# Token sums, first weight splits and the range check's count: three moves in an instruction order

## The chip, the core and the metric

The kernel runs on one core of a Trainium2 chip. Five engines work side by side, each through its own queue in order: PE (TensorE, matrix products), DVE (VectorE), ACT (ScalarE), POOL (GpSimd) and SP (SyncE), which here only starts DMAs. An engine that waits for a semaphore holds up all that stands behind it in its queue. The metric is device time in microseconds (us), the median of several executions; smaller is better. TensorE's clock is granted at one of two levels, 2.4 GHz (1.00 in the views) or 1.2 GHz (0.50).

## What is computed

The reference runs a recurrent attention over 2 x 8 heads of 768 steps, then a feed-forward with an ELU, then four experts that all tokens pass, weighted by shares:

```python
def _moe_ref(x, w_in, w_out):
    h = x @ w_in
    g = np.where(h > 0.0, h, alpha * (np.exp(np.minimum(h, 0.0)) - 1.0))
    return (g @ w_out).astype(np.float32)

def _moe2_ref(x, domain_probs, w1, w2):
    p = domain_probs / (domain_probs.sum(-1, keepdims=True) + 1e-09)
    for e in range(E):
        h = np.maximum(x @ w1[e], 0.0)
        out += p[:, e:e + 1] * (h @ w2[e])
```

There are 1536 tokens of 384 values. The feed-forward is 384 to 2048 to 384; each expert is 384 to 1024 to 384, in float32.

## The kernel before

**Precision.** Every matrix operand is split into a high and a low part: ACT copies the value with rounding (high), DVE or POOL subtracts that from the value (low, line 153). Each product is three passes: high x high, high x low, low x high (`PASSES`). So a matmul that reads a fresh activation waits in its first pass for ACT's copy and in its second for the subtraction.

**The feed-forward** is written as 48 steps, in the hand-written list `ORDER` (lines 67 to 91). Step n takes a quarter of the hidden width (n // 12), a block of 512 tokens (n // 4 % 3) and a slice of 128 hidden values (n % 4). Its tokens: `h` is the first product (9 matmuls, L364, into one bank of PSUM) and ACT's relu and exp on it (L367, L368, into a tile `e` of which there are 2); `e` is DVE's ELU (L372) and ACT's high copy into a tile `hl` (3 of them); `el` is the low part (L153, D on DVE, P on POOL); `z` is the second product (9 matmuls, L384, into three banks); `dr` adds a quarter's sums to the tokens x2 (L393). The last quarter has its dr39, dr43 and dr47 for blocks 0, 1 and 2; these also write the high (ACT) and low (POOL) parts of the new tokens. The first product of a later step needs a bank that an earlier `e` or `dr` has read. Tokens `wl`, `wa`, `wb`, `wc` load and split the feed-forward's weights.

**The experts** follow in `experts`. It gives every piece of work a key, its place in a row of products, and issues all in order of the keys; the feed-forward's last steps (the `lead`, behind the `|` in `ORDER`) are put in with negative keys, 3 for each `h` and `z`. The row begins with `plain`: the first products of two units (u = 0, 1) as 108 matmuls (L577) over blocks 0, 1, 2. From row 36 on the units 2 to 15 take 15 products (L547) each instead of 18, on sums of token blocks and sums of weight blocks; second products (L599) stand between. The sums of tokens are the list `TOKENS` (L527, DVE, 16 of them; "q", "s0", "s2", "v" and six more live in a pool `first` that closes at row `SPREAD`), their high parts L530 (ACT), their low parts L535 or L153. The sums of weight blocks are L465 (POOL, 6 for a unit), their high parts ACT, their low parts POOL (`sums`, L153). The blocks come by DMA into 2 tiles `blocks` (L456).

**The range check.** The program takes each decay chunk's smallest and largest value (L625), compares them with bounds (`judged`, two L629), counts with one small matmul (L631), and a flag decides at the very end whether a slow exact path runs. With these inputs it doesn't.

Of the kernel before, what the change touches and what calls it, by code (L numbers as in the profile page):

```python
# [32 lines left out]
TERMS = 18  # L33
EDGE = 120
AHEAD = 6
SPREAD = 8

# [18 lines left out]
AS_IS = {6: (1, 2), 3: (2, 2), 14: (2, 1)}  # L58
PLACE = {0: 9, 8: 10, 9: 11, 12: 12, 1: 13, 11: 14, 4: 0, 7: 3, 10: 6, 13: 1, 5: 4, 2: 2}


TOKENS = [("q", (1, 1), (2, 1)), (0, "q", (0, 1)), ("s0", (0, 0), (0, 1)), (8, (1, 0), (1, 1)), ("s2", (2, 0), (2, 1)),
          ("v", 8, "s2"), (9, "v", "s0"), (12, 8, (2, 1)), (1, 12, "s0"), (11, 12, (0, 1)),
          (4, 0, (1, 2)), (7, 4, (0, 2)), (10, 9, (2, 2)), (13, "q", (1, 2)), (5, "v", (2, 2)), (2, 10, (0, 2))]


ORDER = """
# [18 lines left out]
z28 z25 h34 wa13D el29P e34 z29 z26 h33 h35 z27 e33 el34P wa28D dr27A h30 z32 wa29D wb13D e35 el33P wb28P z33 wa14D e30  # L86
h31 el35D wb14P wl15 wb29P wc13P wc28D e31 wl31 el30D h36 el31P wc29P z34 wa30D wa15D e36 h40 el36P z30 z35 h41 wb30P
e40 dr35D wc14P wb15D h37 z31 wa31D el40P e37 e41 wb31P wc15P el37P dr31D z40 h42 h38 e38 wc30D el41P e42 h43 z36 e43
z37 h39 wc31P el42P el43P el38D z41 e39 h44 z42 z38 e44 el39D z39 el44D dr39D z43 dr43D h45 e45 h46 el45D z44 e46 h47
el46D z45 e47 z46 el47D z47 dr47A  # L90
""".split()


# [1 line left out]
def kernel_body(ctx, tc, wkr, vv, uu, w_in, w_out, w1, w2, dp, out):  # L95
# [336 lines left out]
    def experts(guard=False, lead=(), switch=None):  # L432
# [5 lines left out]
        def at(key, run, *args):  # L438
            events.append((key, len(events), run, args))
# [187 lines left out]
        def judged():  # L627
            for m, op in enumerate((ALU.is_lt, ALU.is_gt)):
                nc.vector.tensor_single_scalar(ends[:, m], ends[:, m], SAFE[m], op)  # L629
            n = pools["psum"].tile([P, 512], F32, tag="bank", name="chain_n")[0:1, 0:2 * NCH]  # L630
            nc.tensor.matmul(n, lhsT=ones, rhs=ends.rearrange("q a b -> q (a b)"), start=True, stop=True)  # L631
            nc.vector.tensor_reduce(flag, n, mybir.AxisListType.X, ALU.max)


        n, keys = 0, []
# [8 lines left out]
        row = [("plain", f, b, j) for b in range(3) for f in range(4) for j in range(3)]  # L644
# [8 lines left out]
        place = {g: n for n, g in enumerate(row)}  # L653
# [17 lines left out]
        for e in range(4):  # L671
            for b in range(3):
                at(max(SPREAD + 1, place["second", 2 * e, b, 0, 0] - 60), load_share, e, b)
        for u in range(16):
            n = place["product", u, 0] if u > 1 else -20 + 10 * u
            at(n - 75, load_blocks, u)
            if u < 2:
                for i in (0, 3):
                    at(n - 20 + i, split_hi, u, 0, 6, 6, i, 3)
                    at(n - 19 + i, split_lo, u, 0, 6, 6, i, 3)  # L680
                continue
            for i, s in enumerate(SUMS):
                at(n - (50 if u > 2 else 60) + 2 * i, sum_blocks, u, *s)
            for part, at_first, size, k in ((0, 9, 8, n - (34 if u > 2 else 45)), (1, 0, 7, n - 10)):
                for i in (0, 4):
                    at(k + i, split_hi, u, part, at_first, size, i, min(4, size - i))
                    at(k + i + 1.4, split_lo, u, part, at_first, size, i, min(4, size - i))
        for h in range(8):
            n = place["second", h, 0, 0, 0]
# [4 lines left out]
                    at(max(0, n - 37 + 6 * m + 3 * q), second_lo, h, m, q)  # L694
        made = {}
        for i, t in enumerate(TOKENS):
            made[t[0]] = -15.5 + 1.2 * i if i < 10 else 0.5 + 1.1 * (i - 10)
            at(made[t[0]], sum_tokens, i < 10, *t)
        for r, n in PLACE.items():
            k = max(made[r] + 0.7, {0: 11.5, 1: 23.5, 2: 35.5}[n % 3] + 0.9 * (n // 3) if n < 9 else -99)  # L700
            at(k, tokens_hi, r)
# [5 lines left out]

        at(SPREAD, spread_out)
        if guard:
            for c in range(NCH):  # L710
                at(70 + 33 * c - 30, load_guard, c)
                for m in range(2):
                    at(70 + 33 * c + 12 * m, guarded, c, m)
            at(len(row) - 20, judged)
        with tc.manual_schedule():
            for _, _, run, args in sorted(events, key=lambda v: v[:2]):
                run(*args)
# [5 lines left out]
    def switch():  # L723
        m1.close()
        late_pools(late)

    experts(guard=True, lead=ORDER[cut + 1:], switch=switch)
    late.close()
    early.close()
# [32 lines left out]
    with tc.If(some > 0, preferred_fallthrough_block=False):  # L762
        with ExitStack() as es:
            gp = es.enter_context(tc.tile_pool(name="gp", bufs=2))
            sp = es.enter_context(tc.tile_pool(name="sp", bufs=1))
            pools["psum"] = es.enter_context(tc.tile_pool(name="psum", bufs=8, space=PSUM))
            pick = sp.tile([P, 256], F32, name="pick")
            nc.gpsimd.memset(pick, 0.0)
            nc.gpsimd.memset(pick[0:64, 127:128], 1.0)
            nc.gpsimd.memset(pick[64:128, 191:192], 1.0)  # L770
            sts = [sp.tile([P, D, NPAIR], F32, name=f"st{b}") for b in range(2)]
            for st in sts:
                nc.gpsimd.memset(st, 0.0)
            for i in range(NCH):
                recur(i, gp)
        work.clear()
        bank_pool(m0)
        with ExitStack() as es:
            feed_forward_pools(es)
            for q in range(4):  # L780
                do(f"{t}{16 * m + 4 * q + n}" + "D" * (t in ("wa", "wb")) + "P" * (t == "wc") for m in range(2) for n in range(4) for t in ("wl", "wa", "wb", "wc"))
                for n in range(4 * len(BLOCKS) * q, 4 * len(BLOCKS) * (q + 1)):
                    do((f"h{n}", f"e{n}", f"el{n}D", f"z{n}") + (f"dr{n}A",) * (n % 4 == 3))
        with ExitStack() as es:
            early_pools(es)
            late_pools(es)
            experts()
        m0.close()
# [57 lines left out]
```

## Time and profile before

| | us |
|---|---|
| median of 3 runs (684.63 to 685.57) | 685.25 |
| the profiled execution's own time | 684.58 |
| its span | 682.6 |
| PE busy in the span | 641.2 (94%) |
| DVE busy | 498.1 (73%) |
| POOL busy | 397.4 (58%) |
| ACT busy | 304.0 (45%) |

PE is busy in nearly all of the span, so what counts is where it is not, and where it runs at the lower clock. The feed-forward ends, and `plain` begins, at 302.66 us; the sums and the range check are found by their lines.

### The profile page before, as it was taken

How to read it: one execution, taken by the hardware profiler on the slowest of the kernel's cores; microseconds unless marked ns; L12 is line 12 of the kernel's file. 1: busy time of each engine (PE TensorE's matmuls, PEld its weight loads, DVE VectorE, ACT ScalarE, POOL GpSimd, SP SyncE). 2: the span in 40 equal slices, each digit the busy share in tenths (PEclk: the TensorE clock that was granted, in tenths of full speed). 3: DMA queues.
4: the chain of work that ended last, by engine and by line, in shares of the span. 5: the costliest groups of instructions: out<-in, count | busy, mean ns of one | idle time of the engine just before them, and what ended most of it. 6: DMA issues, size and time to landing. Idle time of an engine off the chain costs nothing.

```text
span 682.6 us, 9079 instructions
## 1 busy us (share of the span) xinstructions
PE 641.2 (94%) x3314; PEld 521.6 (76%) x3314; DVE 498.1 (73%) x687; ACT 304.0 (45%) x581; POOL 397.4 (58%) x341
## 2 busy tenths in 40 slices
PE   6768999999999998869999999999999999999994
PEld 4657788888888877648887878878878788788873
DVE  7999997548465653876477687786977877867773
ACT  1334746657564564544552353334423533344220
POOL 5799685325341463873543487675776886744352
PEclk9989999999999999959999999999999999999998
DMA  7665651213211311001202112013121121300012
GB/s 261 193 185 165 213 201 52 61 48 99 64 47 46 99 43 48 23 1 46 86 23 86 31 54 86 15 40 97 44 72 45 34 75 32 115 1 2 0 47 98
DMA packets 20970, 50.83 MB, mean 74 GB/s; under 512 B 2680, under 2 KB 3880, under 8 KB 20916
## 3 DMA queue, kind: packets, MB, share of 16 engines
q1 hardware_dynamic: 20772, 50.15, 23.4%
q8 instruction: 28, 0.46, 0.3%
q14 instruction: 26, 0.21, 0.1%
q10 hardware_dynamic: 144, 0.00, 0.0%
HBM read 46.58 MB, written 2.38 MB: 72 GB/s over the span
## 4 chain that ended last, share of the span: by engine, by line
PE 77%; DVE 10%; POOL 5%; issue 3%; DMA 2%; ACT 1%; SPq 0%; DVEq 0%; POOLq 0%; ACTq 0%
PE second L599 25%; PE bank L364 12%; PE bank L384 12%; PE chain_a L547 8%; PE chain_b L547 4%; PE chain_p L577 4%; PE chain_c L547 3%; PE chain_d L547 3%; DVE scaled L608 2%; DVE first L527 2%; PE bank L292 1%; PE chain_e L547 1%; PE bank L285 1%; POOL kr L150 1%; PE bank L336 1%
## 5 line engine op out<-in xcount | busy, mean ns | idle before, releaser
L599 PE MATMUL second<-hl,w2s 128*128 128x512 f32 x864 | 230.5, 389 | 0.0
L599 PEld LDWEIGHTS second<-hl,w2s 128*128 128x128 f32 x864 | 162.0, 188 | 34.1 <-DVE hl L592 0.2
L613 POOL TENSOR_TENSOR x<-scaled,x 128x512 f32<-128x512 f32 x60 | 84.8, 1439 | 89.4 <-DVE scaled L608 89.4
L384 PE MATMUL bank<-hl,w 128*128 128x512 f32 x432 | 107.8, 400 | 10.2 <-DVE hl L153 7.8
L153 POOL TENSOR_TENSOR sums<-blocks,sums 128x512 fp32r<-128x512 f32 (+1 forms) x60 | 81.3, 1366 | 55.5 <-ACT sums L157 55.5
L384 PEld LDWEIGHTS bank<-hl,w 128*128 128x128 f32 x432 | 81.9, 192 | 29.9 <-DVE hl L153 9.0
L364 PE MATMUL bank<-x,w 128*128 128x512 f32 x432 | 104.0, 391 | 0.5 <-DVE e L372 0.5
L592 DVE SCALAR_TENSOR_TENSOR hl<-terms,hl 128x512 fp32r<-128x512 f32 x96 | 90.6, 947 | 13.3 <-ACT hl L589 13.3
L364 PEld LDWEIGHTS bank<-x,w 128*128 128x128 f32 x432 | 80.4, 188 | 18.6 <-DVE e L372 1.5
L465 POOL TENSOR_TENSOR blocks<-blocks 128x256 f32<-128x256 f32 x84 | 70.9, 861 | 1.7 <-DMA blocks<-in_w 0.6
L153 POOL TENSOR_TENSOR hl<-e,hl 128x512 fp32r<-128x512 f32 x25 | 34.1, 1368 | 56.3 <-ACT hl L157 56.2
L372 DVE SCALAR_TENSOR_TENSOR e<-e,bank 128x512 f32<-128x512 f32 x48 | 32.4, 681 | 43.5 <-ACT e L368 43.5
L589 ACT ACTIVATE hl<-terms 128x512 fp32r<-128x512 f32 x96 | 57.0, 624 | 15.0 <-PE second L599 10.3
L559 DVE TENSOR_TENSOR terms<-terms,chain_a 128x512 f32<-128x512 f32 x42 | 28.7, 684 | 37.9 <-PE chain_a L547 37.9
L562 ACT ACTIVATE terms<-chain_b 128x512 f32<-128x512 f32 x28 | 16.8, 598 | 83.2 <-PE chain_b L547 83.0
L562 ACT ACTIVATE terms<-chain_a 128x512 f32<-128x512 f32 x28 | 16.7, 596 | 78.4 <-PE chain_a L547 78.4
L547 PE MATMUL chain_a<-x,sums 128*128 128x512 f32 x168 | 47.2, 389 | 0.0
L608 DVE TENSOR_TENSOR scaled<-second,pr 128x512 f32<-128x512 f32 x63 | 41.2, 679 | 7.5 <-PE second L599 7.5
L157 ACT ACTIVATE hl<-e 128x512 fp32r<-128x512 f32 x48 | 30.1, 629 | 35.5 <-PE bank L384 22.4
L157 ACT ACTIVATE sums<-blocks 128x512 fp32r<-128x512 f32 (+1 forms) x60 | 35.2, 592 | 13.6 <-POOL sums L153 6.2
L367 ACT ACTIVATE e<-bank 128x512 f32<-128x512 f32 x48 | 28.4, 593 | 26.7 <-PE bank L364 14.2
L547 PEld LDWEIGHTS chain_a<-x,sums 128*128 128x128 f32 x168 | 31.5, 188 | 6.5
(117 smaller groups left out, 1013.2 us busy)
## 6 DMA issues: line engine op xcount, KB each, us to landing
kr<-in_wkr SPq DMA_DIRECT2D x12, 512.0 KB, 4.0
raw<-in_w_in SPq DMA_DIRECT2D x16, 384.0 KB, 3.5
raw<-in_w_out SPq DMA_DIRECT2D x16, 384.0 KB, 3.3
blocks<-in_w SPq DMA_DIRECT2D x16, 384.0 KB, 3.4
raw<-in_w SPq DMA_DIRECT2D x16, 384.0 KB, 4.5
v<-in_vv SPq DMA_DIRECT2D x12, 456.0 KB, 4.4
w<-in_wkr SPq DMA_DIRECT2D x12, 258.5 KB, 3.8
gw<-in_wkr SPq DMA_DIRECT2D x12, 258.0 KB, 2.8
```

Source lines behind the costliest of these rows:

```text
L153: engines[e].tensor_tensor(o, a, b.bitcast(F32), ALU.subtract)
L157: nc.scalar.activation(out=o, in_=a, func=AF.Copy)
L364: nc.tensor.matmul(ph, lhsT=wi[:, sa, f, kk, :], rhs=x[:, kk, c0:c0 + nch, sm], start=(kk == 0 and i == 0), stop=(kk == 2 and i == 2))
L384: nc.tensor.matmul(pxs[q, bl][d], lhsT=wo[:, sa, f, d * P:(d + 1) * P], rhs=b["t"][:, sm], start=(f == 0 and i == 0), stop=(f == 3 and i = ...
L465: nc.gpsimd.tensor_tensor(*(places(blocks[u], p) for p in (r, a, c)), ALU.subtract if op == "-" else ALU.add)
L547: nc.tensor.matmul(banks[c], lhsT=weights(u, r, sa), rhs=tokens(r)[:, sm], start=r in HEADS and i == 0, stop=i == 2, skip_group_check=True)
L562: nc.scalar.activation(out=new({0: 0, 6: 5, 3: 2, 5: 3, 8: 4}[r]), in_=ps, func=AF.Copy, scale=-1.0 if r in (6, 8) else 1.0)
L589: nc.scalar.activation(out=hls[f, b][:, 0], in_=results[f, b], func=AF.Relu)
L592: nc.vector.scalar_tensor_tensor(hls[f, b][:, 1], results[f, b], 0.0, hls[f, b][:, 0].bitcast(F32), ALU.max, ALU.subtract)
L599: nc.tensor.matmul(sums[d], lhsT=w[:, sa, f, d * P:(d + 1) * P], rhs=hls[4 * h + f, b][:, sm], start=f == i == 0, stop=f == 3 and i == 2)
L608: nc.vector.tensor_tensor(o, sums[d], prs[h // 2, b], ALU.mult)
L613: (nc.vector if last else nc.gpsimd).tensor_tensor(x2[:, d, s], scaled[d], x2[:, d, s], ALU.add)
```

## The change

Four numbers or lists move; no operation is added or taken away but a split of one function in two.

- The end of `ORDER`: before, the last first products are h39, h44, h45, h46, h47; now h44, h39, h46, h45, h47, each with a second product between, and block 1's sums (dr43) are taken ahead of block 0's (dr39).
- `TOKENS` begin at key -0.9 instead of -15.5, one each 1.05, and stand in another order; which of them live in the pool `first` is now a set. `SPREAD` goes from 8 to 18.
- Units 0 and 1 split their weights 40 keys earlier (-60 instead of -20), and their DMAs come 40 earlier; unit 2's weight sums go from 60 ahead to 97, its first half's split from 45 to 82, its DMA from 75 to 112.
- The comparisons of the range check go from 20 rows ahead of the end to 26; the count stays at 20.

```diff
-SPREAD = 8
+SPREAD = 18
-TOKENS = [("q", (1, 1), (2, 1)), (0, "q", (0, 1)), ("s0", (0, 0), (0, 1)), (8, (1, 0), (1, 1)), ("s2", (2, 0), (2, 1)),
...
+TOKENS = [("q", (1, 1), (2, 1)), (0, "q", (0, 1)), (4, 0, (1, 2)), (7, 4, (0, 2)), ("s0", (0, 0), (0, 1)),
...
+FIRST = {"q", "s0", "s2", "v", 0, 8, 9, 12, 1, 11}
...
-z37 h39 wc31P el42P el43P el38D z41 e39 h44 z42 z38 e44 el39D z39 el44D dr39D z43 dr43D h45 e45 h46 el45D z44 e46 h47
-el46D z45 e47 z46 el47D z47 dr47A
+z37 h44 wc31P el42P el43P el38D z41 h39 e44 e39 z42 h46 z38 z43 el44D dr43D el39D h45 z44 e45 z39 el45P dr39A e46 h47
+z45 el46D z46 e47 el47D z47 dr47A
...
         def judged():
             for m, op in enumerate((ALU.is_lt, ALU.is_gt)):
                 nc.vector.tensor_single_scalar(ends[:, m], ends[:, m], SAFE[m], op)
+
+        def counted():
             n = pools["psum"].tile([P, 512], F32, tag="bank", name="chain_n")[0:1, 0:2 * NCH]
...
-            n = place["product", u, 0] if u > 1 else -20 + 10 * u
-            at(n - 75, load_blocks, u)
+            n = place["product", u, 0] if u > 1 else -60 + 10 * u
+            at(n - (75 if u != 2 else 112), load_blocks, u)
...
-                at(n - (50 if u > 2 else 60) + 2 * i, sum_blocks, u, *s)
-            for part, at_first, size, k in ((0, 9, 8, n - (34 if u > 2 else 45)), (1, 0, 7, n - 10)):
+                at(n - (50 if u > 2 else 97) + 2 * i, sum_blocks, u, *s)
+            for part, at_first, size, k in ((0, 9, 8, n - (34 if u > 2 else 82)), (1, 0, 7, n - 10)):
...
-            made[t[0]] = -15.5 + 1.2 * i if i < 10 else 0.5 + 1.1 * (i - 10)
-            at(made[t[0]], sum_tokens, i < 10, *t)
+            made[t[0]] = -0.9 + 1.05 * i
+            at(made[t[0]], sum_tokens, t[0] in FIRST, *t)
...
-            at(len(row) - 20, judged)
+            at(len(row) - 26, judged)
+            at(len(row) - 20, counted)
```

DVE at the feed-forward's end, before, right behind step 46's ELU: step 46's low part is hl_2669, step 47's ELU is e_2682 and its low part hl_2713.

```order
L527 TENSOR_TENSOR first_2686<-x2_62 128x512
L527 TENSOR_TENSOR first_2689<-x2_62 128x512
L527 TENSOR_TENSOR first_2693<-first_2686,first_2689 128x512
L153 TENSOR_TENSOR hl_2669<-e_2642,hl_2669 128x512
L527 TENSOR_TENSOR first_2705<-first_2693,first_2666 128x512
L527 TENSOR_TENSOR first_2709<-first_2686,x2_62 128x512
L372 SCALAR_TENSOR_TENSOR e_2682<-e_2682,bank_2672 128x512
L527 TENSOR_TENSOR first_2725<-first_2709,first_2666 128x512
L527 TENSOR_TENSOR first_2729<-first_2709,x2_62 128x512
L535 SCALAR_TENSOR_TENSOR xb_1405<-first_2725,xb_1405 128x512
L535 SCALAR_TENSOR_TENSOR xb_1405<-first_2729,xb_1405 128x512
L153 TENSOR_TENSOR hl_2713<-e_2682,hl_2713 128x512
```

The same stretch of DVE now, from step 39's low part (hl_2566) to the first token sum (step 46 is hl_2669 again, step 47 hl_2704).

```order
L153 TENSOR_TENSOR hl_2566<-e_2556,hl_2566 128x512
L372 SCALAR_TENSOR_TENSOR e_2632<-e_2632,bank_2622 128x512
L393 TENSOR_TENSOR x2_62<-bank_2491,x2_62 128x512
L393 TENSOR_TENSOR x2_62<-bank_2492,x2_62 128x512
L393 TENSOR_TENSOR x2_62<-bank_2493,x2_62 128x512
L372 SCALAR_TENSOR_TENSOR e_2590<-e_2590,bank_2580 128x512
L153 TENSOR_TENSOR hl_2669<-e_2590,hl_2669 128x512
L372 SCALAR_TENSOR_TENSOR e_2682<-e_2682,bank_2672 128x512
L153 TENSOR_TENSOR hl_2704<-e_2682,hl_2704 128x512
L527 TENSOR_TENSOR first_2719<-x2_62 128x512
```

No token sum stands ahead of a low part any more but "q", which now follows the last of them.

POOL some 50 us earlier, before: the low parts of steps 36 (hl_2317), 40 (hl_2367), 37 (hl_2403) and 41 (hl_2406) among weight pieces (raw, w3, w7).

```order
L153 TENSOR_TENSOR hl_2317<-e_2295,hl_2317 128x512
L195 TENSOR_TENSOR raw_2084<-raw_2084,t_2309 128x384
L153 TENSOR_TENSOR w3_1906<-raw_2015,w3_1906 128x384
L153 TENSOR_TENSOR hl_2367<-e_2330,hl_2367 128x512
L195 TENSOR_TENSOR raw_2282<-raw_2282,t_2398 128x384
L153 TENSOR_TENSOR w3_1906<-raw_2273,w3_1906 128x384
L153 TENSOR_TENSOR hl_2403<-e_2386,hl_2403 128x512
L153 TENSOR_TENSOR hl_2406<-e_2362,hl_2406 128x512
```

POOL there now; the steps 36, 40, 37 and 41 are hl_2320, hl_2378, hl_2415 and hl_2418.

```order
L153 TENSOR_TENSOR sums_2309<-blocks_1992,sums_2309 128x384 x2
L153 TENSOR_TENSOR hl_2320<-e_2295,hl_2320 128x512
L153 TENSOR_TENSOR sums_2357<-blocks_2057,sums_2357 128x384
L195 TENSOR_TENSOR raw_2088<-raw_2088,t_2312 128x384
L153 TENSOR_TENSOR w3_1906<-raw_2017,w3_1906 128x384
L153 TENSOR_TENSOR sums_2357<-blocks_2057,sums_2357 128x384
L153 TENSOR_TENSOR hl_2378<-e_2333,hl_2378 128x512
L195 TENSOR_TENSOR raw_2282<-raw_2282,t_2410 128x384
L153 TENSOR_TENSOR w3_1906<-raw_2273,w3_1906 128x384
L153 TENSOR_TENSOR hl_2415<-e_2397,hl_2415 128x512
L465 TENSOR_TENSOR blocks_2359<-blocks_2359 128x256
L465 TENSOR_TENSOR blocks_2359<-blocks_2359 128x2x128
```

Four low parts of the units' weights (sums) came in ahead of step 40's low part, and two weight sums (L465) ahead of step 41's, which is the next row.

DVE at the range check, some 40 second products ahead of the end (- before, + now).

```order
 L608 TENSOR_TENSOR scaled<-second,pr 128x512
 L592 SCALAR_TENSOR_TENSOR hl<-terms,hl 128x512
+L629 TENSOR_SCALAR ends<-ends 128x12 x2
 L608 TENSOR_TENSOR scaled<-second,pr 128x512 x2
 L592 SCALAR_TENSOR_TENSOR hl<-terms,hl 128x512 x2
-L629 TENSOR_SCALAR ends<-ends 128x12 x2
-L632 TENSOR_REDUCE flag<-chain_n 1x1
+L634 TENSOR_REDUCE flag<-chain_n 1x1
```

The two comparisons moved up past two weighted sums (L608) and two low parts (L592); the count on PE stays at its place.

## Rows read from the trace of the kernel before

**Rows 1.** PE in order of time: start, us, instruction; in brackets idle time before it.

```profile
236.25 4.25 PE L384 MATMUL bank<-hl,w 128*128 128x512 f32 x18
240.34 2.21 PE L364 MATMUL bank<-x,w 128*128 128x512 f32 x9
242.85 2.33 PE L364 MATMUL bank<-x,w 128*128 128x512 f32 x9 [0.30 <-DVE e L372]
...
249.10 6.28 PE L364 MATMUL bank<-x,w 128*128 128x512 f32 x27
...
263.71 2.34 PE L364 MATMUL bank<-x,w 128*128 128x512 f32 x9 [0.17 <-DVE e L372]
...
271.99 4.15 PE L384 MATMUL bank<-hl,w 128*128 128x512 f32 x17 [1.64 <-DVE hl L153]
...
287.52 0.49 PE L384 MATMUL bank<-hl,w 128*128 128x512 f32 x1 [1.19 <-ACT hl L157]
289.39 2.94 PE L384 MATMUL bank<-hl,w 128*128 128x512 f32 x8 [1.37 <-DVE hl L153]
293.50 0.79 PE L384 MATMUL bank<-hl,w 128*128 128x512 f32 x1 [1.17 <-ACT hl L157]
299.08 3.78 PE L384 MATMUL bank<-hl,w 128*128 128x512 f32 x8 [4.79 <-DVE hl L153]
302.66 17.64 PE L577 MATMUL chain_p<-x,sums 128*128 128x512 f32 x74
```

**Rows 2.** Windows: length, busy PE, PEld, DVE, ACT, POOL (count), granted clock, DMA share, GB/s.

```profile
270.00:280.00 10.00, 8.36 (x37) 6.66 (x36) 7.13 (x10) 6.39 (x11) 8.30 (x7) 1.00 0.31 103
285.00:290.00 5.00, 2.44 (x10) 1.46 (x10) 4.96 (x8) 2.27 (x4) 2.58 (x3) 1.00 0.00 0
...
295.00:300.00 5.00, 0.92 (x2) 0.82 (x3) 3.93 (x4) 1.15 (x2) 1.67 (x2) 0.50 0.00 0
```

**Rows 3.** DVE in order of time, at the feed-forward's end and in `plain`.

```profile
280.11 0.95 DVE L527 TENSOR_TENSOR first<-x 128x512 f32<-128x512 f32 x1
...
286.73 1.28 DVE L527 TENSOR_TENSOR first<-x 128x512 f32<-128x512 f32 x2
...
297.26 1.77 DVE L153 TENSOR_TENSOR hl<-e,hl 128x512 fp32r<-128x512 f32 x1
...
305.97 1.78 DVE L527 TENSOR_TENSOR terms<-first,x 128x512 f32<-128x512 f32 x1
...
315.07 1.88 DVE L153 TENSOR_TENSOR x<-terms,x 128x512 fp32r<-128x512 f32 x3
```

**Rows 4.** POOL in order of time: a step's low part, a weight piece, unit 0's first splits.

```profile
240.93 1.29 POOL L153 TENSOR_TENSOR hl<-e,hl 128x512 fp32r<-128x512 f32 x1 [3.46 <-ACT hl L157]
242.18 1.02 POOL L195 TENSOR_TENSOR raw<-raw,t 128x384 int32<-128x384 int32 x1
...
266.04 1.99 POOL L153 TENSOR_TENSOR sums<-blocks,sums 128x384 fp32r<-128x384 f32 x2 [0.29 <-ACT sums L157]
```

**Rows 5.** The page's group of weight sums: count, busy us, mean ns, idle before.

```profile
L465 POOL TENSOR_TENSOR blocks<-blocks 128x256 f32<-128x256 f32 x84 | 70.9, 861 | 1.7 <-DMA blocks<-in_w 0.6
```

**Rows 6.** ACT in order of time: a step's exp, and unit 0's first high parts.

```profile
241.37 0.64 ACT L368 ACTIVATE e<-e 128x512 f32<-128x512 f32 x1
...
265.45 0.92 ACT L157 ACTIVATE sums<-blocks 128x384 fp32r<-128x384 f32 x2
```

**Rows 7.** PE at the first second products.

```profile
327.84 4.24 PE L599 MATMUL second<-hl,w2s 128*128 128x512 f32 x18
```

**Rows 8.** The range check: its comparisons on DVE, its count on PE.

```profile
658.26 1.30 DVE L629 TENSOR_SCALAR ends<-ends 128x12 f32<-128x12 f32 x2
...
659.61 0.21 PE L631 MATMUL chain_n<-ends,ones 128*1 128x24 f32 x2 [1.41 <-DVE ends L629]
```

**Rows 9.** A feed-forward weight chunk: its DMA's start on SP, its first use on DVE.

```profile
204.37 0.33 SPq L184 DMA_DIRECT2D raw<-in_w_in  x1
...
215.70 0.35 DVE L189 TENSOR_SCALAR t<-raw 128x384 int32<-128x384 int32 x1
```

More of the change, by code (lines that the diff above doesn't have):

```diff
@@ L59 @@
 PLACE = {0: 9, 8: 10, 9: 11, 12: 12, 1: 13, 11: 14, 4: 0, 7: 3, 10: 6, 13: 1, 5: 4, 2: 2}
-TOKENS = [("q", (1, 1), (2, 1)), (0, "q", (0, 1)), ("s0", (0, 0), (0, 1)), (8, (1, 0), (1, 1)), ("s2", (2, 0), (2, 1)),
-          ("v", 8, "s2"), (9, "v", "s0"), (12, 8, (2, 1)), (1, 12, "s0"), (11, 12, (0, 1)),
-          (4, 0, (1, 2)), (7, 4, (0, 2)), (10, 9, (2, 2)), (13, "q", (1, 2)), (5, "v", (2, 2)), (2, 10, (0, 2))]
+TOKENS = [("q", (1, 1), (2, 1)), (0, "q", (0, 1)), (4, 0, (1, 2)), (7, 4, (0, 2)), ("s0", (0, 0), (0, 1)),
+          (8, (1, 0), (1, 1)), ("s2", (2, 0), (2, 1)), ("v", 8, "s2"), (9, "v", "s0"), (10, 9, (2, 2)),
+          (13, "q", (1, 2)), (5, "v", (2, 2)), (12, 8, (2, 1)), (1, 12, "s0"), (11, 12, (0, 1)), (2, 10, (0, 2))]
+FIRST = {"q", "s0", "s2", "v", 0, 8, 9, 12, 1, 11}
 ORDER = """
```

## The prediction

> **What bounds the kernel now.** PE is busy in 94% of the span, so I looked first at the granted clock and at PE's busy share in slices of time, found one place in mid-kernel where both fall, then read PE in order of time there, and behind each of its waits the engine that ended it. Before 263 us PE's waits are tenths of a microsecond. From there to the first row of `plain` they are 1.64, 1.19, 1.37, 1.17 and 4.79 us, ended by DVE's low parts (L153) and by ACT's copies of ELUs that DVE gave late [rows 1]. In windows PE is busy for 2.44 of 5 us at 285, and 0.92 of 5 at 295 at half clock, while DVE is busy nearly all the time [rows 2]. So here DVE sets the pace, and what it does is sums of tokens (L527), of which the step that PE waits for has no need.
>
> How much is lost? 18 matmuls take 236.25 to 240.34, 0.227 us each, 2.045 for a group of 9 (one `h` or `z`). From 240.34 to `plain` there are 23 groups (h41, h37, z31, z40, then 19 from h42 at 249.10 on), so without any wait `plain` would start at 240.34 + 23 x 2.045 = 287.4. It starts at 302.66 [rows 1]: **15.3 us lost**. The seven waits make 10.6 of that; the matmuls at half clock (8 in 2.94 us, 8 in 3.78, one in 0.79) some 3.2; the rest is restarts.
>
> **Term 1, the old waits: -15.3.** Now no token sum stands between the ELUs and low parts of the last steps; all but one come after them. I walk the tail in the new order. When z39's last bank is done, DVE adds it (0.64), then come step 46's ELU (0.64), ACT's copy (0.7 with its hand-over), step 46's low part, step 47's ELU, ACT's copy and step 47's low part. An unhindered DVE row takes 0.64 (two in 1.28), a low part beside POOL 1.77 [rows 3]; POOL is then at block 0's three low parts, so step 46 gets 1.77, and step 47, behind them, 0.64. Sum 5.7 us. PE wants the last in z47's second matmul, three groups and 0.2 later, 6.3 us: it fits by 0.6. With 1.77 for step 47 too it would be 0.5 late; I take nothing and keep 0.5 as the bound. Each last first product (h39, h46, h45, h47) now also has second products behind it that are ready.
>
> **Term 2, new waits at 246 to 266 us: +3.2.** The price of the earlier weight splits lies on POOL. POOL now has part of the units' splitting ahead of the low parts of steps 40 and 41. ACT's copy of step 36 needs a tile `hl` that z30 frees at 236.25 + 2.05 + 0.1 = 238.4 [rows 1]. Then ACT does that copy, step 40's relu and exp, and a block's high part, 0.46 to 0.64 each, 0.57 apart on the mean [rows 6]: POOL can start the second unit-0 split at 240.7. From there POOL has no pause: split 1.0, step 36's low part 1.3, split 1.0, weight pieces 1.0 and 1.0, split 1.0, step 40's low part 1.3 [rows 4], and ends at 248.3. PE would want it in z40's second matmul, at 240.34 + 3 x 2.045 + 0.23 = 246.7 [rows 1]: **a wait of 1.65**. The old 0.30 at 242.85 is inside this: if it stays, this one is that much shorter. Then h42 wants the bank that step 37's ELU reads; its relu waited for the tile `e` that step 40's low part frees: 248.4 + 2 x 0.6 + 0.7 = 250.4, against 250.2 for z40's end: **0.25**. Then on POOL: a weight piece behind ACT's conversion (250.1 to 251.1), another to 252.1, step 37's low part to 253.4, two weight sums of 0.86 [rows 5] to 255.1, step 41's low part to 256.4. Step 38's relu waits for that, and its ELU comes at 258.5; z36's third bank needs it at 250.4 + 3 x 2.045 + 6 x 0.227 = 257.9: **0.6**. The wait for a bank at h44 (0.17 before, now at h39) stays: **0.2**. Together 2.7; a group behind a wait is 0.12 longer (2.33 against 2.21 [rows 1]), four times 0.5. Bounds: nothing, if ACT and POOL come 1.7 earlier than walked; and 1.1 more, if DVE holds up one of POOL's rows for as long as POOL held up the low part at 297.26 (1.77 - 0.64 [rows 3]).
>
> **Term 3, the clock: -0.6.** `plain` starts at half clock. Its 108 matmuls take 302.66 to 327.84, 25.2 us, against 24.5 at 0.227 [rows 1, 7]. With no long wait ahead of it this goes.
>
> **Term 4, the range check: -1.5.** PE waits 1.41 for the comparisons [rows 8], plus 0.12 for the restart. They now come six rows of three matmuls earlier, 6 x 0.68 = 4.1 us. In exchange the two of them, 1.30 us, stand ahead of two weighted sums and two low parts; those low parts are issued 5.3 rows (3.6 us) before their use. I take nothing for that, with 1.3 as the bound: the place has no row before.
>
> **Term 5, the token sums in their new place: 0, up to +6.2.** They now lie beside `plain`. From the last addition L393 (about 0.9 into `plain`) to the first low part that a second product needs, DVE has 27 rows: 15 sums, 4 low parts of second weights, 8 of tokens. PE gives them 24.5 + 0.2 - 0.9 = 23.8 us, or 0.88 for a row. What does a row take? Unhindered 0.64 [rows 3]. From 305.97 to 316.95 there were 12 in 10.98, 0.915 each; from 280.11 to 299.03 there were 17 in 18.9, 1.11 each; the first and the last of both stand in [rows 3]. The first stretch had POOL busy for about 8 of 11 us. In the new place POOL has six low parts of 1.3 and six weight sums of 0.86, 12.8 of 24 us, so I scale the excess: 0.64 + 0.275 x (0.53 / 0.74) = 0.84. 27 x 0.84 = 22.7: in time by 1.1. At 0.915 it is 0.9 late, at 1.11 it is 6.2 late. I take 0, the price of the nearest row with its cover scaled, and keep 6.2 for the range.
>
> Here the Trainium skill has a rule that speaks against the change. The row first: at 297.26 a subtraction took 1.77 instead of 0.64, 1.13 more, in a stretch in which POOL worked too [rows 3]. The page "SBUF — State Buffer", section "Who interferes with whom", says that a DVE instruction with two SBUF inputs contends with a GpSimd instruction that reads SBUF, and that whoever starts first keeps the shared ports for its whole instruction. By that rule at its worst, each of POOL's 12 instructions beside `plain` would hold up one DVE row by its whole length: 27 x 0.64 + 12.8 = 30.1, 6.3 late, and the sum below would end at 677.4 instead of 671.1. That one row agrees in size; the 12 rows from 305.97, at 0.915, do not show it for each.
>
> **Free edits.** The blocks' DMAs (384 KB) stand earlier on SP, among feed-forward weight chunks. A chunk started at 204.37 is first used at 215.70 [rows 9], 11 us later, which covers a transfer ahead of it; without that cover it would cost the transfer. `SPREAD` only delays the shares' DMA to the row where the pool `first` closes, and its readers come behind the first four second products.
>
> **The sum.** -15.3 + 3.2 - 0.6 - 1.5 + 0 = -14.2. The profiled execution would go from 684.58 to 670.4 (span 682.6 to 668.4); it lies 0.67 under the median of the runs, so the median goes from 685.25 to **671.1**.
>
> **Rivals.**
>
> 1. *The clock falls at the new wait.* PE would stand for 1.65 and 0.25 us within 4 us. For it: at 285 the engine was busy for 2.44 of 5 us, and half clock followed [rows 2]. Against: at 270.4 it waited 1.64 in one piece and the clock stayed at 1.00 [rows 1, 2]. One to three groups at half clock: 2 to 6 us, 673 to 677.
> 2. *DVE stays the bound, beside `plain`.* The sums are only moved to where the second products wait for DVE; the point is a mean row of 0.88 us. Then up to 6.2 comes back: 672 to 677.4. For it the stretch at 1.11, against it the one at 0.915 with more POOL work beside it.
> 3. *Slower than before.* The clock falls at z40 and the small waits that follow (h42, z36, h39) keep it at half up to `plain`: 19 groups x 2.045 = 38.9 more, some 710. It decides from the seventh group on (14.2 / 2.045). Against: behind z40 there would be waits of 0.6 and 0.2 in 16 us, and the window with a wait of 1.64 in it stayed at 1.00; the clock fell behind windows with PE busy for half of the time [rows 2].
> 4. *No new wait at all.* ACT and POOL come early enough at z40: 3.2 less, 668.
>
> **How the numbers follow.** Forecast 0.68, rival 1 0.10, rival 2 0.13, rival 3 0.02, rival 4 0.06, something unseen at either side 0.01. The forecast's own spread is about 1.5 us (term 2's 1.1, term 4's 1.3, term 1's 0.5, not all at once). The range of 668.0 to 676.0 takes in the forecast, rival 4 and most of rivals 1 and 2. A measurement of this kernel tells 0.2%, about 1.4 us, from no change; all but rival 3 are far beyond: faster 0.97, same 0.01, slower 0.02.
>
> **What would show it.** Right: `plain` starts near 290.5, no PE wait over 1 us from 266 to there, granted clock 1.00 throughout; a PE wait of 1 to 2 us near 247 ended by POOL's low part; no wait at the count; first second products 24.5 us after `plain`. Wrong: a wait of PE for DVE's L592 at the first second products (rival 2), a clock under 1.00 behind 247 (rival 1), no wait there (rival 4), or waits in the last six groups (term 1).

## The result and the profile after

The changed kernel takes **676.93 us** (median of 4 runs, 674.91 to 677.39), the kernel before 685.18 in the same comparison: a ratio of 0.9874, 95% interval 0.9853 to 0.9896. It is faster by 8.3 us, where 14.2 were forecast, and lies 0.9 above the range. The profiled execution took 674.91 (span 673.0).

PE in order of time: start, us, instruction, in brackets the idle time ahead of it and what ended it.

```profile
236.48 4.24 PE L384 MATMUL bank<-hl,w 128*128 128x512 f32 x18
...
244.64 2.77 PE L384 MATMUL bank<-hl,w 128*128 128x512 f32 x10
249.41 3.27 PE L384 MATMUL bank<-hl,w 128*128 128x512 f32 x8 [2.00 <-POOL hl L153]
252.48 6.76 PE L364 MATMUL bank<-x,w 128*128 128x512 f32 x27
...
286.01 6.28 PE L384 MATMUL bank<-hl,w 128*128 128x512 f32 x27
292.13 24.64 PE L577 MATMUL chain_p<-x,sums 128*128 128x512 f32 x108
316.97 0.50 PE L599 MATMUL second<-hl,w2s 128*128 128x512 f32 x1 [0.20 <-ACT hl L589]
320.05 4.15 PE L599 MATMUL second<-hl,w2s 128*128 128x512 f32 x17 [2.58 <-DVE hl L592]
324.04 0.84 PE L547 MATMUL chain_d<-x,sums 128*128 128x512 f32 x3
```

The waits of [rows 1] between 270 us and `plain` are gone: `plain` starts at 292.13 instead of 302.66, and the last three groups (27 matmuls) run in one piece. Two waits are left. One was forecast: 2.00 at z40 for POOL's low part of step 40. The other is at the very first second products, 2.58 for DVE.

Windows (length, busy PE, PEld, DVE, ACT, POOL with counts, granted clock, DMA share, GB/s):

```profile
245.00:250.00 5.00, 2.94 (x13) 1.88 (x12) 2.42 (x2) 2.30 (x5) 4.35 (x4) 1.00 0.60 206
250.00:255.00 5.00, 5.00 (x16) 3.93 (x15) 3.08 (x5) 2.79 (x5) 3.77 (x4) 0.66 0.07 25
...
310.00:315.00 5.00, 5.00 (x23) 4.13 (x23) 5.00 (x5) 3.62 (x8) 4.92 (x5) 1.00 0.00 0
315.00:320.00 5.00, 2.28 (x9) 1.31 (x7) 5.00 (x6) 5.00 (x11) 3.56 (x5) 1.00 0.30 100
```

Behind the wait at z40 the granted clock is 0.66 on the mean of 5 us: some of the matmuls ran at half. From 310 to 320 DVE has no pause, as DVE had none at 285 before [rows 2]: the bound has moved along with the sums.

At the program's end PE goes from the last second products into the count without a wait, where there was one of 1.41 [rows 8]:

```profile
637.05 13.08 PE L599 MATMUL second<-hl,w2s 128*128 128x512 f32 x57
650.07 0.21 PE L633 MATMUL chain_n<-ends,ones 128*1 128x24 f32 x2
```

A table that sorts this out, for all kernels run. The work ahead of z30 is nearly the same in all of them, yet its length differs from one execution to the next (z30's first matmul between 235.5 and 239.3 us), so single profiles are best compared from there. Columns: z30's start (z30 is the second product of step 30); from there to `plain`; from `plain` through the first 18 second products to the next product (`chain_d`); from that to the end of the span; the median of the runs. The medians of the kernel before were 685.07, 684.88 and 684.41 beside the three groups of runs (e0 to e3, e4 to e7, e8 and e9); between groups, the ratios to them are the better measure.

| kernel | z30 | to plain | to chain_d | to the end | median of runs |
|---|---|---|---|---|---|
| before | 236.25 | 66.41 | 29.26 | 350.68 | 685.18 |
| the prediction's sum | 236.25 | 54.25 | 28.6 | 349.2 | 671.1 |
| changed | 236.48 | 55.65 | 31.91 | 348.96 | 676.93 |
| e0_after (the same again) | 238.23 | 54.75 | 33.52 | 349.50 | 677.56 |
| e1_unit1_late | 236.94 | 54.33 | 33.48 | 349.15 | 676.36 |
| e2_unit3_late | 236.62 | 54.82 | 29.06 | 349.90 | 671.73 |
| e3_both | 236.93 | 53.99 | 28.97 | 349.61 | 669.81 |
| e4_w2_pool | 238.93 | 54.74 | 34.29 | 349.34 | 678.62 |
| e5_splits_undone | 237.47 | 54.72 | 35.99 | 349.42 | 680.10 |
| e6_guard_only | 238.59 | 66.08 | 28.60 | 348.43 | 682.93 |
| e7_low40_first | 236.61 | 53.95 | 28.96 | 348.98 | 670.90 |
| e8_tokens_only | 239.34 | 54.09 | 34.81 | 350.26 | 679.49 |
| e9_old_order | 235.50 | 59.61 | 33.52 | 349.27 | 680.41 |

The third column is where the forecast went: 31.9 to 33.5 instead of 28.6.

### The profile page after: what moved, and what is told of

Read it like the earlier page. It is cut to its first block, busy times and chain, and to the rows that moved or that the text cites. A ratio compares the mean times of both kernels' runs of the same rounds, so it can differ in the third digit from the quotient of the medians.

```text
span 673.0 us, 9079 instructions
## 1 busy us (share of the span) xinstructions
PE 639.1 (95%) x3314; PEld 521.0 (77%) x3314; DVE 498.2 (74%) x686; ACT 302.7 (45%) x581; POOL 397.9 (59%) x342
## 3 DMA queue, kind: packets, MB, share of 16 engines
q1 hardware_dynamic: 20772, 50.15, 23.8%
## 4 chain that ended last, share of the span: by engine, by line
PE 51%; DVE 8%; issue 2%; ACT 1%; POOL 0%; DVEq 0%
PE second L599 26%; PE chain_a L547 8%; PE chain_b L547 4%; PE bank L384 3%; PE chain_c L547 3%; PE chain_d L547 3%; PE bank L364 2%; DVE scaled L608 2%; PE chain_e L547 1%; DVE first L527 1%; DVE terms L559 1%; DVE hl L592 1%; DVE terms L527 1%; DVE ends L625 1%; DVE terms L564 0%
## 5 line engine op out<-in xcount | busy, mean ns | idle before, releaser
L384 PE MATMUL bank<-hl,w 128*128 128x512 f32 x432 | 105.7, 395 | 2.1 <-POOL hl L153 2.0
L153 POOL TENSOR_TENSOR sums<-blocks,sums 128x512 fp32r<-128x512 f32 (+1 forms) x60 | 82.1, 1378 | 41.6 <-ACT sums L157 41.5
L592 DVE SCALAR_TENSOR_TENSOR hl<-terms,hl 128x512 fp32r<-128x512 f32 x96 | 91.8, 960 | 8.7 <-ACT hl L589 8.7
L465 POOL TENSOR_TENSOR blocks<-blocks 128x256 f32<-128x256 f32 x84 | 69.0, 838 | 1.2
L153 POOL TENSOR_TENSOR hl<-e,hl 128x512 fp32r<-128x512 f32 x26 | 35.5, 1366 | 48.6 <-ACT hl L157 48.0
L608 DVE TENSOR_TENSOR scaled<-second,pr 128x512 f32<-128x512 f32 x63 | 41.2, 679 | 5.6 <-PE second L599 5.6
L367 ACT ACTIVATE e<-bank 128x512 f32<-128x512 f32 x48 | 28.4, 593 | 29.0 <-POOL hl L153 12.8
```

The source lines that it names most:

```text
L153: engines[e].tensor_tensor(o, a, b.bitcast(F32), ALU.subtract)
L384: nc.tensor.matmul(pxs[q, bl][d], lhsT=wo[:, sa, f, d * P:(d + 1) * P], rhs=b["t"][:, sm], start=(f == 0 and i == 0), stop=(f == 3 and i = ...
L465: nc.gpsimd.tensor_tensor(*(places(blocks[u], p) for p in (r, a, c)), ALU.subtract if op == "-" else ALU.add)
L592: nc.vector.scalar_tensor_tensor(hls[f, b][:, 1], results[f, b], 0.0, hls[f, b][:, 0].bitcast(F32), ALU.max, ALU.subtract)
L608: nc.vector.tensor_tensor(o, sums[d], prs[h // 2, b], ALU.mult)
```

## The experiments

**Why the second products wait.** Theory: beside `plain`, POOL's work makes DVE's rows long. DVE in the changed kernel, then POOL:

```profile
294.14 1.23 DVE L153 TENSOR_TENSOR w2s<-raw,w2s 128x384 fp32r<-128x384 f32 x1 [1.11 <-ACT w2s L157]
...
308.73 0.68 DVE L527 TENSOR_TENSOR first<-first 128x512 f32<-128x512 f32 x1
309.42 1.70 DVE L153 TENSOR_TENSOR x<-terms,x 128x512 fp32r<-128x512 f32 x1
311.04 1.23 DVE L527 TENSOR_TENSOR first<-first,x 128x512 f32<-128x512 f32 x1
...
314.48 1.23 DVE L527 TENSOR_TENSOR terms<-terms,x 128x512 f32<-128x512 f32 x1
...
319.32 1.28 DVE L592 SCALAR_TENSOR_TENSOR hl<-terms,hl 128x512 fp32r<-128x512 f32 x2
```

```profile
308.95 1.62 POOL L153 TENSOR_TENSOR xb<-first,xb 128x512 fp32r<-128x512 f32 x1 [2.50 <-ACT xb L530]
310.53 6.64 POOL L465 TENSOR_TENSOR blocks<-blocks 128x256 f32<-128x256 f32 x6
```

A row that began just ahead of POOL's low part of 308.95 takes 0.68, the one begun beside it 1.70 (it ends 0.55 after POOL's row), and rows beside the weight sums 1.23. Those six sums are unit 3's, whose first product stands 36 rows, some 24 us, behind the first second product. The run e2 moves them (and their splitting) out:

```diff
-                at(n - (50 if u > 2 else 97) + 2 * i, sum_blocks, u, *s)
-            for part, at_first, size, k in ((0, 9, 8, n - (34 if u > 2 else 82)), ...
+                at(n - (97, 36, 50)[min(u, 4) - 2] + 2 * i, sum_blocks, u, *s)
+            for part, at_first, size, k in ((0, 9, 8, n - (82, 22, 34)[min(u, 4) - 2]), ...
```

> The changed kernel, but unit 3's six weight sums on POOL and their splitting come 14 and 12 rows later, out of the stretch in which DVE does the token sums. Theory 1, that POOL's work makes DVE's rows longer (1.22 us each beside the weight sums at 310 to 317, 0.64 to 0.68 alone): DVE's rows there go to about 0.7, the wait of 2.58 falls under 0.5, 674.9 - 2.5 = 672.4 profiled; the wait at z40 stays near 2.0. Rival, that DVE's rows are long because of something of their own or of ACT's pace: wait stays above 2, time within 0.5 of the changed kernel.

Measured: 671.73 (670.63 to 672.34), against 677.56 for the changed kernel on the same chip, 5.8 less. DVE in the same stretch, and PE at the second products:

```profile
310.36 0.68 DVE L527 TENSOR_TENSOR first<-first,x 128x512 f32<-128x512 f32 x1
310.96 0.68 DVE L153 TENSOR_TENSOR x<-terms,x 128x512 fp32r<-128x512 f32 x1
311.56 0.68 DVE L535 SCALAR_TENSOR_TENSOR xb<-first,xb 128x512 fp32r<-128x512 f32 x1
312.16 0.68 DVE L527 TENSOR_TENSOR terms<-terms,x 128x512 f32<-128x512 f32 x1
```

```profile
291.44 24.65 PE L577 MATMUL chain_p<-x,sums 128*128 128x512 f32 x108
...
316.48 4.19 PE L599 MATMUL second<-hl,w2s 128*128 128x512 f32 x17 [0.15 <-DVE hl L592]
```

With POOL idle, every one of these rows is 0.68 instead of 1.23, DVE gets there in time, and the wait is 0.15. DVE's 27 rows take 21.6 us instead of 25.2. The theory holds. The gain of the medians is more than the wait itself. Between the profiles of e2 and of the changed kernel beside it (e0, below) 4.46 lies at the second products, the wait and 1.6 of half clock behind it; another 1.61 lies ahead of z30, where the two programs do the same.

The counter-test e4 gives POOL more: four low parts of second weights (L153, `w2s`) move from DVE to it.

```diff
-            sub("D", w2s[h][:, 1, s], raws[h, m][:, DM * q:DM * q + DM], w2s[h][:, 0, s])
+            sub("D" if h else "P", w2s[h][:, 1, s], raws[h, m][:, DM * q:DM * q + DM], w2s[h][:, 0, s])
```

> The changed kernel, but the four low parts of the first second weights (w2s) are subtracted on POOL instead of DVE. Theory 1, that DVE's rows beside plain are made long by POOL's work: DVE loses four rows (1.23 and three of 0.55, 2.9 us) and a pause of 1.11 for ACT's copy, but POOL's four new rows of about 1.0 each make DVE's rows beside them longer by 0.5 to 1.1; the wait of 2.58 at the first second products falls to between 0.5 and 2, and the profiled time by 0.6 to 2. Rival, that a row's length on DVE doesn't depend on POOL: the whole 4 us goes, no wait is left there, 2.6 us and the half clock behind it less.

Measured: 678.62 (677.04 to 679.59). DVE has four rows fewer and still comes later: 23 rows from 294.48 to 321.93, 1.19 each, against 27 in 25.2, 0.93 each. Three sums that took 2.99 beside a single POOL row now take

```profile
306.52 3.71 DVE L527 TENSOR_TENSOR terms<-first,x 128x512 f32<-128x512 f32 x3
```

and the first second products wait 1.28 and 2.57:

```profile
319.59 0.50 PE L599 MATMUL second<-hl,w2s 128*128 128x512 f32 x1 [1.28 <-ACT hl L589]
322.66 5.46 PE L599 MATMUL second<-hl,w2s 128*128 128x512 f32 x17 [2.57 <-DVE hl L592]
```

Counted from the start of `plain`, the first low part (L592) begins 28.3 us on, against 27.2 in the changed kernel. By its ratio the kernel is as fast as that one (0.9894 against 0.989 in e0). Neither number forecast came true: the theory named the right cause and still set its price too low.

**The same kernel again.** No edit.

> The changed kernel once more, unchanged, as the neighbour of the next three on the same chip, and to see what its slower executions hold: its profiled run took 674.91 us, three others 676.6 to 677.4. Theory 1: how long TensorE's clock stays at half behind the wait of 2.00 us at z40 (about 249 us) differs from run to run; a profile of a slower run then shows more matmuls at half clock there, by about 2 us. Theory 2: the first second products wait longer for DVE than 2.58 us in the slower runs; the clock rows are then equal.

Measured: 677.56 (677.02 to 677.97), profiled 677.87. Its PE rows at the same two places:

```profile
251.18 2.11 PE L384 MATMUL bank<-hl,w 128*128 128x512 f32 x8 [2.01 <-POOL hl L153]
...
320.90 5.76 PE L599 MATMUL second<-hl,w2s 128*128 128x512 f32 x17 [2.58 <-DVE hl L592]
```

The waits are the same to 0.01. But 8 matmuls behind z40's wait take 2.11 here and 3.27 above, and 17 behind the other take 5.76 here and 4.15 above; the window 320 to 325 is granted 0.66. So in each of these two executions half clock followed one of the two waits, a different one, at 1.2 and 1.6 us. Both theories were wrong in part: the place changes, not only the length. Of the 3.0 us between the two spans 1.75 lie ahead of z30, -0.9 at the first wait, 1.6 at the second and 0.5 behind it. It is no rule that one of the two is hit: e9, below, shows half clock behind both and behind a third wait, and e2 none behind a wait of the same length at z40:

```profile
249.56 2.11 PE L384 MATMUL bank<-hl,w 128*128 128x512 f32 x8 [2.00 <-POOL hl L153]
```

With the second wait gone (e2, e3, e7) none of the three profiles shows half clock at either place. What decides it stays open.

**The wait at z40.** POOL in the changed kernel, from unit 0's second split on:

```profile
241.19 1.02 POOL L153 TENSOR_TENSOR sums<-blocks,sums 128x384 fp32r<-128x384 f32 x1 [2.08 <-ACT sums L157]
242.17 1.30 POOL L153 TENSOR_TENSOR hl<-e,hl 128x512 fp32r<-128x512 f32 x1
243.42 1.33 POOL L153 TENSOR_TENSOR sums<-blocks,sums 128x384 fp32r<-128x384 f32 x1
...
246.70 1.11 POOL L153 TENSOR_TENSOR sums<-blocks,sums 128x384 fp32r<-128x384 f32 x1
247.78 1.57 POOL L153 TENSOR_TENSOR hl<-e,hl 128x512 fp32r<-128x512 f32 x1
```

The last is step 40's low part. The two splits between are unit 1's; e1 puts them back where they were.

```diff
-            n = place["product", u, 0] if u > 1 else -60 + 10 * u
+            n = place["product", u, 0] if u > 1 else (-60, -10)[u]
```

> The changed kernel, but unit 1's weights are split where they were before (two splits leave POOL's row ahead of step 40's low part; units 0 and 2 stay early). Theory 1, that POOL's row of splits makes the wait at z40: the wait of 2.00 falls under 0.4, no half clock behind it, plain starts near 288.3 instead of 292.13, and the profiled time is 674.9 - 3.8 = 671.1, the median under 672. The wait of 2.58 at the first second products stays as it is. Rival, that another chain (ACT's copies, the tile e) ends at the same time: 1 us or more of the wait stays, 673 to 675.

Measured: 676.36 (675.9 to 676.77), 1.2 under the changed kernel beside it. The wait falls to 0.85, no half clock follows it, and the other stays at 2.59, with half clock behind it as in e0:

```profile
249.03 2.09 PE L384 MATMUL bank<-hl,w 128*128 128x512 f32 x8 [0.85 <-POOL hl L153]
...
319.16 5.76 PE L599 MATMUL second<-hl,w2s 128*128 128x512 f32 x17 [2.59 <-DVE hl L592]
```

So the splits made more than half of the wait and something else the rest. The time expected was missed twice over: to `plain` only 1.3 of the 3.8 came off the first profile of the changed kernel (55.65 to 54.33), and the 1.6 of half clock at the second products, which that profile did not have, is in this one. Both edits together:

> Both edits of the two runs before together. If the two losses are independent, 674.9 - 3.8 - 2.5 = 668.6 profiled and a median near 669; if one wait takes the place of the other (DVE's lateness at the first second products grows when plain starts earlier), about 671.

Measured: **669.81** (669.1 to 671.28), ratio 0.9775 to the kernel before, interval 0.975 to 0.9801. This beats both kernels. To `plain` 53.99, to `chain_d` 28.97: close to the prediction's sum at each. The run e7 goes for the 0.85 that is left; it adds to e3:

```diff
-... z30 z35 h41 wb30P
-e40 dr35D wc14P wb15D h37 z31 wa31D el40P e37 ...
+... z30 z35 e40
+h41 dr35D el40P wc14P wb15D h37 z31 wb30P wa31D e37 ...
```

> The kernel with both edits (unit 1 split late, unit 3's sums late) and, in the feed-forward's order, step 40's ELU and low part ahead of the weight pieces that stood before them on ACT and POOL. Theory 1, that the 0.85 us left at z40 is POOL's and ACT's weight pieces ahead of the low part: no wait of over 0.3 at z40, plain about 0.9 to 1.0 earlier, and the time 0.9 under that kernel's median of 669.8. Rival, that the pieces set back come late for the products that read them, or step 37's ELU or the bank it holds: a wait of the same size a few groups later, no gain.

Measured: 670.90 (670.2 to 673.64). The wait at z40 is gone, and two stand a few groups on. The one of 0.67 is new; at the place of the other, z36, e3 already lost 0.4 (18 matmuls in 4.62 instead of 4.24). The weight piece set back on POOL (L195) holds up DVE's next piece (L189), and behind that stand the ELUs that free the banks. PE, then DVE:

```profile
250.09 6.46 PE L364 MATMUL bank<-x,w 128*128 128x512 f32 x27 [0.67 <-DVE e L372]
...
258.33 3.02 PE L384 MATMUL bank<-hl,w 128*128 128x512 f32 x12 [0.43 <-DVE e L372]
```

```profile
248.48 0.36 DVE L189 TENSOR_SCALAR t<-raw 128x384 int32<-128x384 int32 x1 [3.17 <-POOL raw L195]
...
249.35 1.28 DVE L372 SCALAR_TENSOR_TENSOR e<-e,bank 128x512 f32<-128x512 f32 x2
```

To `plain` it is 53.95 against 53.99: no gain, as the rival said.

**What each part of the change is worth.** e5 undoes the earlier splits of units 0, 1 and 2, and keeps the rest.

```diff
-            n = place["product", u, 0] if u > 1 else -60 + 10 * u
-            at(n - (75 if u != 2 else 112), load_blocks, u)
+            n = place["product", u, 0] if u > 1 else -20 + 10 * u
+            at(n - 75, load_blocks, u)
...
-                at(n - (50 if u > 2 else 97) + 2 * i, sum_blocks, u, *s)
+                at(n - (50 if u > 2 else 60) + 2 * i, sum_blocks, u, *s)
...
```

> The changed kernel with the weights of units 0, 1 and 2 loaded, summed and split where they were before (the new order of the feed-forward, the token sums and the range check stay). Theory 1, that POOL's early rows buy room for the last steps: the wait at z40 goes (2.0), but unit 2's six sums and two splits (7 us on POOL) now stand among the low parts of block 1's and block 0's tokens and of step 45: waits of 2 us or more between 275 us and plain or at its start, and more of DVE's rows beside plain lie beside POOL; 676 to 682. Rival, that POOL has room for them there: without the wait at z40 some 673 to 675.

Measured: 680.10 (678.13 to 680.69). No wait at z40, but POOL now does unit 2's sums ahead of step 45's low part, and more of them beside DVE:

```profile
285.91 6.44 PE L384 MATMUL bank<-hl,w 128*128 128x512 f32 x26 [2.02 <-POOL hl L153]
...
318.87 0.50 PE L599 MATMUL second<-hl,w2s 128*128 128x512 f32 x1 [2.03 <-ACT hl L589]
321.93 6.42 PE L599 MATMUL second<-hl,w2s 128*128 128x512 f32 x17 [2.56 <-DVE hl L592]
```

So the early splits, with the wait they bring, are worth some 2 us: 2.5 by the medians, 1.8 by the ratios (0.9917 against 0.989 in e0), whose intervals just overlap. e8 makes the change in the token sums alone (`TOKENS`, their keys, `FIRST`, `SPREAD`), everything else as before:

> The kernel before with the token sums alone moved (list, keys, the pool they live in); feed-forward order, splits and range check as before. Theory 1, that the sums ahead of the last steps' rows on DVE are what cost the 15.3 us: the waits of 1.19, 1.37, 1.17 and 4.79 and the half clock around them go (some 11 to 12 us), the wait of 1.64 at 272 stays or shrinks, and 4 to 5 us come back at the first second products, as with the splits undone (waits 2.0 and 2.6): 676 to 681 for the median. Rival, that the order of the last first products is what makes the waits: 2 us or more of waits stay in the last steps, over 682.

Measured: 679.49 (677.71 to 681.01), 4.9 less than before. All waits from 287 us to `plain` are gone, with the old order of the last first products; the one of 1.64 at 272 stays (this kernel's line numbers are one higher):

```profile
275.16 4.15 PE L385 MATMUL bank<-hl,w 128*128 128x512 f32 x17 [1.64 <-DVE hl L154]
...
287.31 6.28 PE L385 MATMUL bank<-hl,w 128*128 128x512 f32 x27
```

The stretch to `plain` falls from 66.41 to 54.09, and 5.5 us of the 12.3 come back at the second products (29.26 to 34.81). e9 is the changed kernel with the old end of `ORDER`:

> The changed kernel with the end of the feed-forward's order as before (sums, splits and range check new). Theory 1, that the new order of the last first products buys the last of the wait: against the changed kernel's 677.3 it is 1.6 to 4 slower (the wait of 1.64 for step 39's or 41's low part, and step 47's, which has one product less ahead of it). Rival, that with the sums gone the old order is as good: within 0.5 of it.

Measured: 680.41 (679.93 to 681.01), ratio 0.9945 against 0.989 in e0: 2.9 us more by the medians, 3.8 by the ratios. The wait at z39 is back, and in this execution half clock follows it, and also z40's wait and the one at the second products, so a part of the loss is the clock's:

```profile
248.45 3.58 PE L384 MATMUL bank<-hl,w 128*128 128x512 f32 x8 [2.00 <-POOL hl L153]
...
275.22 5.76 PE L384 MATMUL bank<-hl,w 128*128 128x512 f32 x17 [2.02 <-DVE hl L153]
...
323.02 5.76 PE L599 MATMUL second<-hl,w2s 128*128 128x512 f32 x17 [2.57 <-DVE hl L592]
```

e6 is the kernel before with the range check's part alone:

```diff
-            at(len(row) - 20, judged)
+            at(len(row) - 26, judged)
+            at(len(row) - 20, counted)
```

> The kernel before with only the range check's comparisons moved six rows ahead of the count. Theory: PE's wait of 1.41 at the count and its restart of 0.1 go, and nothing takes their place: 1.5 less than the kernel before. Rival: the two comparisons (1.30 us) stand ahead of two low parts that second products need, and up to 1.3 of waits comes back there: 0.2 less.

Measured: 682.93 against 684.88, ratio 0.9974, interval 0.9958 to 0.9991: 0.6 to 2.9 less, in accord with the 1.5. PE shows no wait at the count.

## Why the prediction was wrong

Of the 5.8 us by which the forecast of the median missed, 3.3 lie at the second products (term 5), 1.4 ahead of `plain` (z40's longer wait and the half clock behind it), and 1.3 are the median's greater distance from its profiled execution; the end is 0.2 shorter. By the prediction's own steps, against the profiled execution (673.0 of span, 668.4 forecast):

- **Term 1 (-15.3) was right.** No wait of the last steps is left from 266 us to `plain`; the tail that was walked fits, step 47's low part included. e8 and e9 divide the term: the sums take the waits from 287 on, the order takes the one at 272.
- **Term 2 (+3.2) was right in place and mechanism.** 1.65 was forecast at z40, 2.00 came. The 0.25 at h42 and 0.6 at z36 do not show in this execution, in which PE was slowed by half clock first; without it, in e0, those rows are 0.2 and 0.4 longer than the same matmuls without a wait (27 in 6.46, 18 in 4.62). To `plain` the kernel took 55.65 with some half clock behind z40 and 54.75 without; forecast 54.25. So rival 1 was real, but with about 1 us, under the 2 to 6 that it named, and in one of the two executions that have a trace.
- **Term 3 (-0.6) and the free edits held.** `plain` takes 24.64 (25.2 less 24.5 is 0.7, a slip of 0.1); no wait for a DMA grew: DVE's longest for a weight chunk between 190 and 262 us was 3.64 and is 1.01.
- **Term 4 (-1.5) was right.** From `chain_d` to the end: 350.68 before, 348.96 now; e6 alone agrees.
- **Term 5 (0) failed; it is rival 2 that happened.** The wait of PE for L592 is the sign that the prediction had named for it. It took 2.58, with 0.2 ahead of it and, in e0, 1.6 of half clock behind it: 31.9 to 33.5 in place of 28.6. Four things were mis-sized or left out. The row: 0.93 on the mean, not 0.84. The start: DVE's first row came 1.11 after the last addition, because ACT copied block 2's three new high parts ahead of the weights that the row needs; that pause was not in the sum. And the cover of POOL: some 15 of DVE's 25.2 us (from the rows of POOL, 0.59), not 12.8 of 24 (0.53), as POOL's rows, too, are longer beside DVE's (1.11 a weight sum, where 0.86 was taken [rows 5]). And the low part itself (L592, 0.64) is a row more than the 27 counted. From the last addition's end, 293.02, the sum 1.11 + 25.2 + 0.64 leads to 319.97; PE's first matmul of the second products had ended at 317.47, and PE went on at 320.05: the wait of 2.58.

The scaling itself was the weak step. A mean over a stretch [rows 3] times POOL's share of busy time hides that the price is one by one: a DVE row beside a weight sum costs 0.55 more, beside a low part 1.0 more. Both prices stood in the trace of the kernel before: the 1.77 of [rows 3] beside a low part, and this row beside four weight sums (DVE, then POOL):

```profile
284.98 1.23 DVE L535 SCALAR_TENSOR_TENSOR x<-first,x 128x512 fp32r<-128x512 f32 x1
```

```profile
282.18 4.62 POOL L465 TENSOR_TENSOR blocks<-blocks 128x256 f32<-128x256 f32 x4
```

An estimate in hindsight from these pairs, six at 1.0 and six at 0.55 on top of 27 rows of 0.64, is 26.6 us, 2.8 over the 23.8 of the forecast. It would have shown, too, that the six sums at the end of the stretch belong to a unit that wasn't in need. The rule of the Trainium skill ("SBUF — State Buffer", section "Who interferes with whom") pointed there: its worst case, every POOL row holding up DVE by its whole length, gave 6.3 late and 677.4. The rows agree with it in kind; the price is under that worst case: 0.55 for a weight sum that itself took 1.11, 1.0 for a low part of 1.62.

Two counts in the term are off as well. From 280.11 to 299.03 DVE has 18 rows, not 17, so 1.05 each, and the upper bound is 4.6 late instead of 6.2 (675.8 instead of 677.4 in rival 2). Six rows of 1.3 and six of 0.86 make 13.0, not 12.8, which changes nothing.

- **The median** lies 2.0 above the profiled execution, not 0.67 as before. The two traced executions of this program had half clock behind different waits, at 1.2 and 1.6; which of the 4 runs had which is not known, as only one of them has a trace, and what makes the rest of the distance stays open.
- **The range** was cut at 676.0, inside rival 2 (672 to 677.4), which had 0.13; a term whose bounds were 0 and 6.2, with a margin of 1.1 on its value, deserved the whole of it. With the wait taken away (e2) the median is 671.73, 0.6 from the forecast. That is closer than the sum deserves: e2's profiled span is 670.4 against 668.4, each of its four stretches 0.4 to 0.7 longer than in the sum, and its median happens to lie 0.6 under the profiled time (672.34) instead of 0.67 over it.

## What to carry to other kernels

Work taken off the path of one engine must be counted again where it lands, row by row against what the neighbouring engines do there, and not by a mean from another stretch. Where DVE and POOL both work from SBUF in a stretch that DVE bounds, look first for POOL work there that isn't needed yet: moving six weight sums and their splitting later gave 5.8 us here by the medians, of which the profiles place 2.9 to 4.5 at the products that waited. And a wait of 2 us on PE cost up to 3.2, one of 2.58 up to 4.2, where half clock followed it.

## What the runs showed of the hardware

Moving four subtractions from DVE to POOL made DVE's stretch longer than keeping them: 23 rows took 27.4 us with POOL's four extra rows, 27 rows took 25.2 without them (e4 and the changed kernel). And half clock behind a wait was not decided by the wait's length alone: behind 2.00 to 2.01 us at z40 the next 8 matmuls took 3.27 in one execution and 2.11 in another, of the same program; behind 2.58 at the second products the next 17 took 4.15 and 5.76.
